# Top-k attention and a Fourier-mix MLP on one core: batch 1's fold in one go, and batch 0's MLP ended before it

## The chip, the cores and the metric

One NeuronCore of a Trainium2 chip runs the whole kernel. The metric is the device time of one execution in microseconds. The kernel before took 2009.99 us, the median of 3 runs (2008.93 to 2011.29).

## What is computed

The reference is cut here to what matters. Attention keeps, in each row of scores, the 32 largest; its output, bridged to (8, 576, 512), goes through a real-valued two-dimensional Fourier transform, a normalisation and an MLP.

```python
# attention: q, k, v are (8, 8, 576, 64), float32
scores = (1 / sqrt(64)) * q @ k.transpose(0, 1, 3, 2)
kth    = np.partition(scores, -32, axis=-1)[..., -32:-31]
scores = np.where(scores >= kth, scores, -1e9)
attn   = softmax(scores)
x      = (attn @ v).transpose(0, 2, 1, 3).reshape(8, 576, 512)

# Fourier mix and MLP: w_ch1 is (512, 2048), w_ch2 is (2048, 512)
mixed = real(fft(fft(x, axis=1), axis=2))
u     = x + mixed
un    = (u - mean(u)) / sqrt(var(u) + 1e-6)
out   = u + maximum(un @ w_ch1, 0) @ w_ch2
```

## The kernel before

The order of all instructions is fixed by a plan in steps. A step stands for one tile of 128 rows of scores of one head (64 rows of two heads in the tail tile): 9 tiles make a pair of heads, 4 pairs a batch, so a batch has 36 steps and the attention 288. In step i, TensorE computes the scores of tile i+3 and transposes the masked exponentials of tile i-2; VectorE finds the 32 largest of tile i in four rounds of MAX8 with three MATCH_REPLACE8 between them, two rounds of tile i beside two of tile i+1; GpSimd and ScalarE build the mask and the exponential.

```python
def top_ops(i, rounds):                       # VectorE; S and wk are tiles of 128 x 576
    for r in rounds:
        src, m8 = s if r == 0 else w, m[:, 8 * r:8 * r + 8]
        nc.vector.max(out=m8, in_=src)
        if r < TOPK // 8 - 1:
            nc.vector.match_replace(w, m8, src, NEG)

def mask(i):
    nc.scalar.activation(out=w, in_=Ssb[i], func=AF.Relu, scale=-FAR, bias=Nt[i][:, 1:2])
    nc.gpsimd.tensor_tensor(out=w, in0=Ssb.pop(i), in1=w, op=ALU.subtract)
```

When the four pairs of a batch are through, its rows x (288 + 288 rows in 5 tiles, the last with 64 tail rows) are folded by symmetry, once for each parity of the frequencies. A fold is a sum or difference of the two halves (first), a fold of the columns (second) and another with a reversed half (third). The 32 tail rows of the second half have to be moved to other partitions first (moved).

```python
def moved():
    out, in_ = place(0)[0:TH, 2, :], x[TH:TAIL, 4, :]
    if eng[1] is nc.vector and eng[0] is nc.vector:
        nc.vector.tensor_copy(out=out, in_=in_)
    else:
        nc.scalar.copy(out=out, in_=in_)

def first(p):      # p 0: 128 x 1024, engine eng[0];  p 1: 32 x 512, engine eng[1], needs moved()
    ...
def second(p):     # two instructions: 128 x 512 (p 0) or 32 x 256 (p 1), engine mid or eng[p]
    ...
def third(n, p):   # two additions each, 128 x 254 (p 0) or 32 x 127 (p 1), engine eng[p]
    ...
```

The buffers of a fold are "own" (two tags, fold_s and fold_d) or the space "hT", which otherwise holds the hidden layer of the MLP. dft_tokens(b, par) is then the transform over the tokens on TensorE, one call for each parity; dft_channels(b, t) that over the channels, one call for each of the 5 tiles; add_mixed (GpSimd), stats and rsqrt (VectorE and GpSimd) and channels_first (transposes) prepare the MLP.

The MLP of a batch is a queue of 68 units of TensorE work: 16 units of the first layer (hidden) for each of two chunks of rows, and 36 of the second layer (back; 4 matmuls of 128 x 512 in the profile's records, lines 771 and 807). The units are spread over the steps up to the time when the next batch's MLP arrives:

```python
def level(i):
    steps = range(i, next((a for a in arrivals if a > i), i + PER_BATCH))
    rest, lev = sum(u[0] for u in queue + held), 0.0
    while lev < 6.4 and sum(max(0.0, lev - fixed_cost(s)) for s in steps) < rest:
        lev += 0.02
    return lev        # planned TensorE time of a step
```

In the main loop a step fills its room up to that level with units. For batch 1 (soon) the plan is:

```python
T0 = end + (2 if first else 3 if soon else 4)          # 74 for batch 1
...
elif soon:
    for par in range(2):
        def folds(par=par, b=b, T1=T0 + 1 + 3 * par):
            f = fold_ops(b, par, (nc.gpsimd, nc.vector), mid=nc.vector)
            at(T1 if par else T1 - 1, "act", f["moved"])
            at(T1, "pool0", lambda: f["first"](0))
            at(T1, "dve", lambda: [
                f["first"](1), f["second"](0), f["second"](1),
                f["third"](0, 1), f["third"](1, 1),
            ])
            at(T1 + 1, "pool0", lambda: [f["third"](n, 0) for n in range(2)])
        at(T0, "begin", folds)
    ft, fc = (T0 + 3, T0 + 6), T0 + 7                   # transforms at 77 and 80, channels from 81
```

Of the kernel before, what the change touches and what calls it, by code (L numbers as in the profile page):

```python
# [59 lines left out]
def kernel(  # L60
# [9 lines left out]
    nc = tc.nc  # L70
# [196 lines left out]
    PER_BATCH = NPB * PER_PAIR  # L267
# [232 lines left out]
    Q1, Q2, Q3 = DM // 4, DM // 2, 3 * DM // 4  # L500
    ROWS3 = (P, P, TH)
    PARTS = [(slice(0, P), slice(0, 2)), (slice(0, TH), slice(2, 3))]
    folded, y_of, yt_of, us_of, rs_of, unT_of = ({} for _ in range(6))

    def fold_ops(b, par, eng, space="own", mid=None):

        x = x_of[b]

        if space == "hT":
            sp = batp.tile([P, NIT * CW[0]], F32, name=f"fsp_{b}", tag="hT")

        def buf(n, name):
            if space == "hT":
                return sp[:, 3 * DM * n:3 * DM * (n + 1)].rearrange("p (s c) -> p s c", s=3)
            pool, tag = (batp, ("fold_s", "fold_d")) if space == "own" else (attp, ("PT0", "PT1"))
            return pool.tile([P, 3, DM], F32, name=f"{name}_{b}_{par}", tag=tag[n % 2], bufs=1)  # L520

        got = folded[b, par] = []

        def place(n):
            while len(got) <= n:
                got.append(buf(len(got), ("sd", "zw", "fg")[len(got)]))
            return got[n]

        def moved():

            out, in_ = place(0)[0:TH, 2, :], x[TH:TAIL, 4, :]
            if eng[1] is nc.vector and eng[0] is nc.vector:
                nc.vector.tensor_copy(out=out, in_=in_)
            else:
                nc.scalar.copy(out=out, in_=in_)

        def first(p):
            sd, op = place(0), ALU.add if par == 0 else ALU.subtract
            if p == 0:
                eng[0].tensor_tensor(out=sd[:, 0:2, :], in0=x[:, 0:2, :], in1=x[:, 2:4, :], op=op)  # L540
            else:
                s_ = sd[0:TH, 2, :]
                eng[1].tensor_tensor(out=s_, in0=x[0:TH, 4, :], in1=s_, op=op)

        def second(p):
            pp, ss = PARTS[p]
            s_, z_ = place(0)[pp, ss], place(1)[pp, ss]
            for cols, op in ((slice(0, Q2), ALU.add), (slice(Q2, DM), ALU.subtract)):
                (mid or eng[p]).tensor_tensor(
                    out=z_[:, :, cols], in0=s_[:, :, 0:Q2], in1=s_[:, :, Q2:DM], op=op  # L550
                )

        def third(n, p):
            pp, ss = PARTS[p]
            z_, f_ = place(1)[pp, ss], place(2)[pp, ss]

            def tt(out, up, down, op):
                eng[p].tensor_tensor(out=f_[:, :, out], in0=z_[:, :, up], in1=z_[:, :, down], op=op)

            if n == 0:  # L560
                eng[p].memset(f_[:, :, Q1:Q1 + 1], 0.0)
                eng[p].tensor_copy(out=f_[:, :, 0:DM:Q2], in_=z_[:, :, 0:DM:Q2])
                up, down = slice(1, Q1), slice(Q2 - 1, Q1, -1)
                tt(up, up, down, ALU.add)
                tt(slice(Q1 + 1, Q2), up, down, ALU.subtract)
            else:
                up, down = slice(Q2 + 1, Q3), slice(DM - 1, Q3, -1)
                tt(up, up, down, ALU.subtract)
                tt(slice(Q3, DM - 1), up, down, ALU.add)
                eng[p].tensor_copy(out=f_[:, :, DM - 1:DM], in_=z_[:, :, Q3:Q3 + 1])  # L570

        return {"moved": moved, "first": first, "second": second, "third": third}

    def fold_steps(f):

        def one():
            f["moved"]()
            f["first"](0)
            f["first"](1)

        def two():
            f["second"](0)
            f["second"](1)

        def three(n):
            f["third"](n, 0)
            f["third"](n, 1)

        return [one, two, lambda: three(0), lambda: three(1)]

    def dft_tokens(b, par):

        while any(u[2] == "hidden" for u in queue):
            one_unit()
        _, zw, fg = folded[b, par]
        if b not in y_of:
            y_of[b] = batp.tile([P, 4, S], F32, name=f"y_{b}", tag="y")
        y = y_of[b]
        yps = [
            ps_m.tile([P, 2, KQ], F32, name=f"yp_{b}_{par}_{g2}", tag="mm") for g2 in range(2)  # L600
        ]

        def mm(g2, gg, st, lhsT, rows, table, start=False):

            nc.tensor.matmul(  # L605
                yps[g2][0:rows, gg, :],
                lhsT=lhsT[0:ROWS3[st]],
                rhs=fs[0:ROWS3[st], table, par, st, :],
                start=start,
                stop=st == 2,  # L610
                skip_group_check=True,
            )

        for g2 in range(2):
            for gg in range(2):
                g = 2 * g2 + gg
                for st in range(2):
                    mm(  # L620
                        g2, gg, st, fg[:, st, P * g:P * (g + 1)], P, gg,
                        start=gg == 0 and st == 0,
                    )
        for st in range(3):
            mm(0, 1, st, zw[:, st, Q1:Q1 + 1], 1, 0)
        for g2 in range(2):
            for gg in range(2):
                g = 2 * g2 + gg
                mm(g2, gg, 2, fg[:, 2, P * g:P * (g + 1)], P, gg)

        mir, back = (
            (slice(HS + 2, S, 2), slice(KQ - 2, 0, -1)) if par == 0
            else (slice(HS + 1, S, 2), slice(KQ - 2, None, -1))
        )
        for g2, yp in enumerate(yps):
            y2 = y[:, 2 * g2:2 * g2 + 2, :]
            nc.scalar.copy(out=y2[:, :, par:HS + 1:2], in_=yp[:, :, 0:KQ - par])
            nc.scalar.copy(out=y2[:, 0, mir], in_=yp[:, 0, back])
            nc.scalar.mul(out=y2[:, 1, mir], in_=yp[:, 1, back], mul=sg[:, g2:g2 + 1])
        if par == 1:  # L640
            tails_of_y(b)
        return 4.3

# [228 lines left out]
    prep("k", 0)  # L872


    plan, costs, arrivals = {}, {}, []

    def at(step, where, fn, cost=0.0):
        plan.setdefault((step, where), []).append(fn)
# [51 lines left out]
    for b in range(B):  # L930
# [3 lines left out]
        T0 = end + (2 if first else 3 if soon else 4)  # L934
        if first:

            def folds(b=b):
                for par, space in ((0, "own"), (1, "hT")):
                    for op in fold_steps(fold_ops(b, par, (nc.vector, nc.vector), space)):
                        op()  # L940
            at(T0, "dve", folds)
            ft, fc = (T0 + 1, T0 + 1), T0 + 1
        elif soon:

            for par in range(2):
                def folds(par=par, b=b, T1=T0 + 1 + 3 * par):
                    f = fold_ops(b, par, (nc.gpsimd, nc.vector), mid=nc.vector)
                    at(T1 if par else T1 - 1, "act", f["moved"])
                    at(T1, "pool0", lambda: f["first"](0))
                    at(T1, "dve", lambda: [  # L950
                        f["first"](1), f["second"](0), f["second"](1),
                        f["third"](0, 1), f["third"](1, 1),
                    ])
                    at(T1 + 1, "pool0", lambda: [f["third"](n, 0) for n in range(2)])
                at(T0, "begin", folds)
            ft, fc = (T0 + 3, T0 + 6), T0 + 7
        elif not last:
            for par in range(2):
                def folds(par=par, b=b, T0=T0):
# [12 lines left out]
            at(ft[par], "pe1", lambda b=b, par=par: dft_tokens(b, par), 4.3)  # L972
        for n, t in enumerate((0, 1, 4, 2, 3)):
            quick = first or last
            s = fc + (0 if first else n // 3 if last else n // 2)
            at(s, "pe2", lambda b=b, t=t, q=quick: dft_channels(b, t, q), 1.75)
            if not quick:
                at(s, "pool2", lambda b=b, t=t: add_mixed(b, t))
                at(s + 1, "dve", lambda b=b, t=t: stats(b, t))
            at(s + (1 if quick else 2), "pe", lambda b=b, t=t: channels_first(b, t), 0.6)  # L980
            if first and t == 4:
                at(s + 1, "pe", lambda: (queue.extend(held), held.clear()) and 0.0)
        at(s + 1, "begin" if quick else "dve", lambda b=b: rsqrt(b))
        arrivals.append(s + (1 if quick else 2))
        at(arrivals[-1], "units", lambda b=b: (queue if b else held).extend(mlp_units(b)))

    queue, held, pending, written, now, out_next = [], [], [], set(), [0], []
    step_us = 6.0
# [12 lines left out]

    def level(i):

        steps = range(i, next((a for a in arrivals if a > i), i + PER_BATCH))
        rest, lev = sum(u[0] for u in queue + held), 0.0
        while lev < 6.4 and sum(max(0.0, lev - fixed_cost(s)) for s in steps) < rest:
            lev += 0.02
# [6 lines left out]
    def one_unit():  # L1014
        c, fn, _ = queue.pop(0)
        fn()
        return c
# [160 lines left out]
```

## Time and profile before

| | |
|---|---|
| span of the profiled execution | 2010.3 us, 27513 instructions |
| TensorE (PE) busy | 1863.9 us, 93% |
| VectorE (DVE) busy | 1641.2 us, 82% |
| ScalarE (ACT) busy | 1220.3 us, 61% |
| GpSimd (POOL) busy | 831.2 us, 41% |
| DMA | 29 GB/s mean |
| attention, steps 0 to 287 | until about 1790 us; then the last batch's transform and MLP |

How to read it: the busy share is an average over stages that differ. Until about 300 us there is no MLP to run and TensorE has gaps; after 1790 us VectorE has nearly nothing to do. Between these, TensorE and VectorE are both busy nearly all the time, so what a stage is bound by has to be read from windows of that stage, and from how far TensorE's step lags behind VectorE's. PEld is the load of weights, beside the matmuls.

### The profile page before, as it was taken

What the parts mean: (1) busy time and instruction counts of PE and PEld (TensorE: products, weight loads), DVE (VectorE), ACT (ScalarE), POOL (GpSimd) and SP (SyncE); (2) the same over time, 40 slices, a digit from 0 to 9 for tenths busy, and PEclk for the clock granted to TensorE, in tenths of its full rate; (3) what the DMA queues carried; (4) which work ended last, traced back from release to release, by engine and by line L of the source; (5) the groups of instructions that cost most, each with busy time, mean ns of one, the idle gap of its engine ahead of it and who ended that gap; (6) DMA issues with size and microseconds to landing.
All of it is one profiled execution on the core that took longest, in us unless ns stands there. A gap on an engine that the chain in (4) does not pass through costs nothing.

```text
span 2010.3 us, 27513 instructions
## 1 busy us (share of the span) xinstructions
PE 1863.9 (93%) x8626; PEld 1126.1 (56%) x8626; DVE 1641.2 (82%) x3405; ACT 1220.3 (61%) x3008; POOL 831.2 (41%) x1114
## 2 busy tenths in 40 slices
PE   5666679999889999999999999999999999998999
PEld 2333356465555656647565656647565656565655
DVE  7999889999999998988889888988899888853100
ACT  6878737677666766656665667656666667541100
POOL 4779822333433365234532374225533364223000
PEclk9678679999999999999999999999999999998999
DMA  4323100010000100001000001010000001000000
GB/s 128 96 82 100 54 7 19 24 26 24 23 19 24 27 24 24 18 18 26 24 24 13 26 19 29 18 32 18 19 24 24 23 15 30 0 14 1 11 14 11
DMA packets 133584, 57.81 MB, mean 29 GB/s; under 512 B 124352, under 2 KB 124480, under 8 KB 133440
## 3 DMA queue, kind: packets, MB, share of 16 engines
q1 hardware_dynamic: 132208, 55.73, 10.3%
q8 instruction: 69, 1.13, 0.2%
q14 instruction: 75, 0.61, 0.1%
q10 hardware_dynamic: 1232, 0.33, 0.1%
HBM read 46.57 MB, written 9.44 MB: 28 GB/s over the span
## 4 chain that ended last, share of the span: by engine, by line
PE 69%; DVE 12%; POOL 6%; ACT 6%; issue 6%; DMA 0%; SPq 0%; POOLq 0%; DVEq 0%
PE cp L771 20%; PE hp L747 20%; PE o L430 7%; PE sp L328 5%; PE tpP L393 5%; DVE m L349 5%; DVE wk L351 4%; PE yp L605 3%; POOL wk L366 3%; PE cp L807 2%; PE mp L661 2%; PE sp_t L298 1%; POOL w L192 1%; ACT wk L365 1%; ACT wk L372 1%
## 5 line engine op out<-in xcount | busy, mean ns | idle before, releaser
L366 POOL TENSOR_TENSOR wk<-S,wk 128x576 f32<-128x576 f32 x288 | 406.9, 1413 | 864.9 <-ACT wk L365 833.6
L349 DVE MAX8 m<-wk 128x8 f32<-128x576 f32 x864 | 623.1, 749 | 5.4
L747 PE MATMUL hp<-unT,w 128*128 128x256 f32 (+1 forms) x2048 | 538.3, 409 | 3.7 <-POOL t L709 2.2
L771 PE MATMUL cp<-w,hT 128*128 128x512 f32 x1024 | 479.3, 600 | 0.0
L747 PEld LDWEIGHTS hp<-unT,w 128*128 128x128 f32 x2048 | 372.7, 190 | 128.2 <-issue 32.2
L351 DVE MATCH_REPLACE8 wk<-m,wk 128x576 f32<-128x576 f32 x576 | 427.6, 742 | 0.0
L771 PEld LDWEIGHTS cp<-w,hT 128*128 128x128 f32 x1024 | 179.6, 190 | 183.6 <-issue 182.8
L372 ACT ACTIVATE wk<-wk,nt 128x576 f32<-128x576 f32 x288 | 225.0, 781 | 79.2 <-POOL wk L366 77.8
L365 ACT ACTIVATE wk<-S,nt 128x576 f32<-128x576 f32 x288 | 226.3, 786 | 50.0 <-POOL nt L358 47.8
L393 PE MATMUL tpP<-ident,wk 128*128 128x128 f32 x1152 | 186.8, 287 | 73.0 <-ACT wk L372 38.0
L396 ACT COPY PT<-tpP 128x512 f32<-128x512 f32 (+1 forms) x320 | 170.7, 544 | 117.4 <-PE tpP L393 114.9
L349 DVE MAX8 m<-S 128x8 f32<-128x576 f32 x288 | 214.1, 743 | 32.8 <-ACT S L302 32.5
L393 PEld LDWEIGHTS tpP<-ident,wk 128*128 128x128 f32 x1152 | 140.3, 146 | 174.2 <-ACT wk L372 56.7
L751 ACT ACTIVATE hT<-hp 128x320 f32<-128x320 f32 (+1 forms) x256 | 104.6, 409 | 192.2 <-PE hp L747 190.0
L351 DVE MATCH_REPLACE8 wk<-m,S 128x576 f32<-128x576 f32 x288 | 213.7, 742 | 0.0
L430 PE MATMUL o<-PT,v 128*64 128x256 f32 (+3 forms) x1440 | 195.9, 414 | 4.6 <-ACT PT L396 4.1
L331 ACT COPY S<-sp 128x512 f32<-128x512 f32 (+1 forms) x264 | 141.9, 588 | 73.3 <-PE sp L328 73.0
L328 PE MATMUL sp<-kT,qT 64*128 64x512 f32 (+1 forms) x528 | 168.1, 690 | 2.3 <-ACT means L922 1.9
L430 PEld LDWEIGHTS o<-PT,v 128*64 128x64 f32 x1440 | 111.5, 153 | 78.1 <-issue 14.6
L192 POOL TENSOR_TENSOR w<-w,space 128x512 f32<-128x512 f32 x96 | 123.6, 1287 | 8.6 <-ACT space L183 5.7
L785 DVE SCALAR_TENSOR_TENSOR x<-cp,gi,x 128x512 f32<-128x512 f32 x11 | 8.2, 746 | 128.3 <-PE cp L771 128.3
L479 DVE TENSOR_TENSOR x<-tpx,rd 128x256 f32<-128x256 f32 x64 | 27.1, 424 | 73.7 <-PE tpx L475 71.0
(125 smaller groups left out, 1899.0 us busy)
## 6 DMA issues: line engine op xcount, KB each, us to landing
space<-in_moe_w_ch_dram SPq DMA_DIRECT2D x32, 512.0 KB, 3.5
nat<-in_q_dram SPq DMA_DIRECT2D x128, 64.0 KB, 2.0
v<-in_v_dram SPq DMA_DIRECT2D x128, 64.0 KB, 2.1
out_dram<-x SPq DMA_DIRECT2D x32, 256.0 KB, 2.1
nat<-in_k_dram SPq DMA_DIRECT2D x124, 64.0 KB, 2.1
nat<-in_q_dram SPq DMA_DIRECT2D x128, 8.0 KB, 1.7
v<-in_v_dram SPq DMA_DIRECT2D x128, 8.0 KB, 1.7
nat<-in_k_dram SPq DMA_DIRECT2D x124, 8.0 KB, 1.7
```

The source lines that it names most:

```text
L192: nc.gpsimd.tensor_tensor(out=dst, in0=dst, in1=(low, high, ex)[part], op=ALU.mult if part else ALU.add,)
L328: nc.tensor.matmul(sp[r], lhsT=qT[hd, q_cols], rhs=kT[hd, :], start=True, stop=True)
L349: ops.append(lambda src=src, m8=m8: nc.vector.max(out=m8, in_=src))
L351: ops.append(lambda src=src, m8=m8: nc.vector.match_replace(w, m8, src, NEG))
L365: nc.scalar.activation(out=w, in_=Ssb[i], func=AF.Relu, scale=-FAR, bias=Nt[i][:, 1:2])
L366: nc.gpsimd.tensor_tensor(out=w, in0=Ssb.pop(i), in1=w, op=ALU.subtract)
L372: nc.scalar.activation(out=w, in_=w, func=AF.Exp, bias=Nt.pop(i)[:, 0:1], accum_out=den_t[pair % 3][:, c:c + 1],)
L393: nc.tensor.transpose(tp[:, c, :], p_sb[:, k0 + P * c:k0 + P * (c + 1)], ident)
L396: nc.scalar.copy(out=pt[:, NF * he:NF * (he + 1), col:col + w], in_=tp[:, :, o:o + w])
L430: nc.tensor.matmul(o[D * e:D * (e + 1), c0:c1], lhsT=vv[:, c, e, :], rhs=pt[:, 2 * NF if c == NF else NF * e + c, c0:c1], start=(c == 0), ...
L747: nc.tensor.matmul(hp[:, 0:w], lhsT=w1[:, dt, P * it:P * (it + 1)], rhs=unT[:, dt, 0:w], start=(dt == 0), stop=(dt == NDT - 1),)
L771: nc.tensor.matmul(cp, lhsT=hT[:, it, P * n:P * (n + 1)], rhs=w2[:, it, :], start=(it == 0), stop=(it == NIT - 1),)
```

## The change

It touches the stage around batch 1's fold, some 40 steps on each side of step 74.

- Batch 1's two parities are folded in one go from step 74: parity 1 wholly on VectorE, in the hT space; parity 0 in step 75, shared with GpSimd as before. Their token transforms stand at steps 76 and 77, the channel transforms at 78 and 79.
- For that, hT has to be free at step 74: batch 0's MLP is spread over the steps up to 74 (a new list, ends, takes the place of arrivals in level), and what is left of it is emptied at the start of that step.
- Batch 1's MLP starts at step 80, with the first chunk of rows, instead of 85.
- moved() is always on ScalarE. This concerns both folds of batch 0 and one of the last batch; the others had it there already.
- The tails of y are taken when both parities are done, whichever comes last.

The purpose is to close the stretch around batch 1's fold in which TensorE has too little to do.

The diff, cut to its core:

```diff
         def moved():
             out, in_ = place(0)[0:TH, 2, :], x[TH:TAIL, 4, :]
-            if eng[1] is nc.vector and eng[0] is nc.vector:
-                nc.vector.tensor_copy(out=out, in_=in_)
-            else:
-                nc.scalar.copy(out=out, in_=in_)
+            nc.scalar.copy(out=out, in_=in_)
...
         if first:
-            def folds(b=b):
+            def folds(b=b, T0=T0):
                 for par, space in ((0, "own"), (1, "hT")):
-                    for op in fold_steps(fold_ops(b, par, (nc.vector, nc.vector), space)):
-                        op()
-            at(T0, "dve", folds)
+                    f = fold_ops(b, par, (nc.vector,) * 2, space)
+                    at(T0, "act", f["moved"])
+                    for op in fold_steps(f, False):
+                        at(T0, "dve", op)
+            at(T0, "begin", folds)
...
         elif soon:
-            for par in range(2):
-                def folds(par=par, b=b, T1=T0 + 1 + 3 * par):
-                    ...
-            ft, fc = (T0 + 3, T0 + 6), T0 + 7
+            def folds(b=b, T0=T0):
+                while queue:
+                    one_unit()
+                f = [
+                    fold_ops(b, 0, (nc.gpsimd, nc.vector), "own", nc.vector),
+                    fold_ops(b, 1, (nc.vector,) * 2, "hT"),
+                ]
+                for n in (1, 0):
+                    at(T0, "act", f[n]["moved"])
+                for op in fold_steps(f[1], False):
+                    at(T0, "dve", op)
+                at(T0 + 1, "pool0", lambda: f[0]["first"](0))
+                at(T0 + 1, "dve", lambda: [
+                    f[0]["first"](1), f[0]["second"](0), f[0]["second"](1),
+                    f[0]["third"](0, 1), f[0]["third"](1, 1),
+                ])
+                at(T0 + 2, "pool0", lambda: [f[0]["third"](n, 0) for n in range(2)])
+            at(T0, "begin", folds)
+            ft, fc = (T0 + 3, T0 + 2), T0 + 4
...
-            s = fc + (0 if first else n // 3 if last else n // 2)
+            s = fc + (0 if first else n // 3 if soon or last else n // 2)
...
-            if first and t == 4:
-                at(s + 1, "pe", lambda: (queue.extend(held), held.clear()) and 0.0)
+            if (first or soon) and t == 4:
+                ready = s + (1 if first else 2)
+                at(ready, "pe", lambda: (queue.extend(held), held.clear()) and 0.0)
...
-        arrivals.append(s + (1 if quick else 2))
-        at(arrivals[-1], "units", lambda b=b: (queue if b else held).extend(mlp_units(b)))
+        arrivals.append(ready if first or soon else s + (1 if quick else 2))
+        at(arrivals[-1], "units", lambda b=b: (queue if b > 1 else held).extend(mlp_units(b)))
+        ends.append(T0 if soon else arrivals[-1])
...
     def level(i):
-        steps = range(i, next((a for a in arrivals if a > i), i + PER_BATCH))
+        steps = range(i, next((a for a in ends if a > i), i + PER_BATCH))
```

More of the change, by code (lines that the diff above doesn't have):

```diff
@@ L502 @@
     PARTS = [(slice(0, P), slice(0, 2)), (slice(0, TH), slice(2, 3))]
-    folded, y_of, yt_of, us_of, rs_of, unT_of = ({} for _ in range(6))
+    folded, y_of, done_of, yt_of, us_of, rs_of, unT_of = ({} for _ in range(7))
     def fold_ops(b, par, eng, space="own", mid=None):
@@ L572, in fold_ops, with fold_steps @@
         return {"moved": moved, "first": first, "second": second, "third": third}
-    def fold_steps(f):
+    def fold_steps(f, moved=True):
         def one():
-            f["moved"]()
+            if moved:
+                f["moved"]()
             f["first"](0)
@@ L639, in dft_tokens @@
             nc.scalar.mul(out=y2[:, 1, mir], in_=yp[:, 1, back], mul=sg[:, g2:g2 + 1])
-        if par == 1:
+        done_of.setdefault(b, set()).add(par)
+        if len(done_of[b]) == 2:
             tails_of_y(b)
@@ L872 @@
     prep("k", 0)
-    plan, costs, arrivals = {}, {}, []
+    plan, costs, arrivals, ends = {}, {}, [], []
     def at(step, where, fn, cost=0.0):
@@ L935 @@
         if first:
-            def folds(b=b):
+            def folds(b=b, T0=T0):
                 for par, space in ((0, "own"), (1, "hT")):
-                    for op in fold_steps(fold_ops(b, par, (nc.vector, nc.vector), space)):
-                        op()
-            at(T0, "dve", folds)
+                    f = fold_ops(b, par, (nc.vector,) * 2, space)
[3 more added lines that the diff above has]
+            at(T0, "begin", folds)
             ft, fc = (T0 + 1, T0 + 1), T0 + 1
         elif soon:
-            for par in range(2):
-                def folds(par=par, b=b, T1=T0 + 1 + 3 * par):
[L947 to L955, printed above, removed]
-            ft, fc = (T0 + 3, T0 + 6), T0 + 7
+            def folds(b=b, T0=T0):
[17 more added lines that the diff above has]
+            ft, fc = (T0 + 3, T0 + 2), T0 + 4
         elif not last:
```

## The prediction

> **What bounds the kernel now.** I read the shares of busy time first, then the groups, then the windows cut at the edges of the plan's steps, then the timelines of VectorE, TensorE and GpSimd around batch 1's fold. From the page:
>
> ```profile
> PE 1863.9 (93%) x8626; PEld 1126.1 (56%) x8626; DVE 1641.2 (82%) x3405; ACT 1220.3 (61%) x3008; POOL 831.2 (41%) x1114
> ...
> L349 DVE MAX8 m<-wk 128x8 f32<-128x576 f32 x864 | 623.1, 749 | 5.4
> ...
> L351 DVE MATCH_REPLACE8 wk<-m,wk 128x576 f32<-128x576 f32 x576 | 427.6, 742 | 0.0
> ```
>
> TensorE looks like the bound for the whole span. But each step of the plan needs four MAX8 and three MATCH_REPLACE8 on VectorE; these seven with their value loads take 5.08 us, the distance from one tile's first MAX8 on S to the next tile's in an undisturbed stretch of VectorE's timeline (316.7 to 321.8 us). So the question is which engine bounds the steps that the change touches. I take the start of a step as that first MAX8: step 39 starts at 298.5, step 74 at 487.5, step 80 at 531.5, step 85 at 563.5, step 123 at 769.5, step 127 at 799.9. Busy time between these edges (columns: stretch, length, PE, PEld, DVE, ACT, POOL, granted clock, DMA):
>
> ```profile
> 298.50:487.50 189.00, 186.65 (x898) 111.64 (x900) 183.05 (x379) 132.22 (x332) 61.41 (x87) 1.00 0.10 23
> 487.50:531.50 44.00, 38.66 (x179) 22.05 (x175) 43.50 (x90) 25.69 (x67) 22.34 (x29) 0.92 0.08 20
> 531.50:563.50 32.00, 29.35 (x164) 20.82 (x165) 31.38 (x72) 22.26 (x54) 13.02 (x16) 1.00 0.07 19
> 563.50:769.50 206.00, 199.66 (x938) 116.37 (x938) 199.04 (x408) 137.47 (x349) 88.76 (x131) 0.98 0.10 23
> 769.50:799.90 30.40, 27.56 (x169) 19.67 (x168) 25.99 (x60) 23.76 (x63) 14.39 (x17) 1.00 0.15 36
> ```
>
> In the second and third rows, batch 1's fold and transform, TensorE idles 5.3 + 2.7 us while VectorE idles 0.5 + 0.6: VectorE is the bound there. In the first row VectorE idles 6.0 of 189.0, and 2.5 of that is the 0.07 us that every step loses. Only from batch 2 on does TensorE bound: over steps 163 to 198 (1018.6 to 1240.9) it is busy 220.6 of 222.3 us and VectorE 193.7.
>
> VectorE's timeline at batch 0's two folds:
>
> ```profile
> 267.80 3.15 DVE L549 TENSOR_TENSOR zw<-sd 128x512 f32<-128x512 f32 x4
> ...
> 276.91 1.95 DVE L549 TENSOR_TENSOR fsp<-fsp 128x512 f32<-128x512 f32 x4
> ```
>
> and at the first of batch 1's:
>
> ```profile
> 499.18 3.17 DVE L549 TENSOR_TENSOR zw<-sd 128x512 f32<-128x512 f32 x4
> ```
>
> The same four instructions take 1.95 us alone and 3.15 to 3.17 when a GpSimd subtraction (1.4 to 2.1 us, in GpSimd's timeline at 268.2 and 499.6) lies beside them. And the largest bubble of TensorE here, in its timeline, at step 86:
>
> ```profile
> 571.36 1.11 PE L393 MATMUL tpP<-ident,wk 128*128 128x128 f32 x4 [5.62 <-ACT kT L257]
> ```
>
> GpSimd's timeline shows what lies behind it: the sixteen small instructions of rsqrt run from 563.0 to 567.3, and the mask's subtraction of step 84 stands behind them, then the exponential, then this transpose.
>
> **What the Trainium skill says.** "Perfetto Trace Analysis", section "Identifying the Most-Contended Engine", calls a busy share of matmuls a poor measure and occupancy a fair one for VectorE; the five windows agree, since TensorE at 97% (199.66 of 206.00) goes with steps of 5.1 us set by VectorE. "SBUF — State Buffer", section "Who interferes with whom", says that a tensor_tensor with both inputs in SBUF contends with GpSimd for a shared port and that the loser blocks; the 1.95 against 3.15 us agree. "TensorE: Matmul & The Clock Gate", Part 1, says that the clock halves after an idle stretch; the trace grants 0.50 in step 86, during the bubble shown above, and 0.92 over the second window.
>
> **The change part by part.** First a yardstick. The plan's own unit costs give TensorE 169.0 us for steps 40 to 72; its first score matmul of step 40 starts at 307.8 and that of step 73 at 480.2, 172.4 us. For steps 88 to 121 it is 183.4 against 187.1. So TensorE needs 1.02 times the plan's costs when nothing holds it.
>
> *Batch 0's MLP ends by step 72 instead of 78.* Before, 28 matmul records of line 771 follow 487.5 in TensorE's timeline: 7 units of 4 records, at 3.44 us per 8 about 12 us. The change moves them ahead of step 74. Followed step by step, the plan gives TensorE 184.8 us for steps 40 to 72, so TensorE starts step 73 at 307.8 + 184.8 x 1.02 = 496.3, 16.1 later. Before, TensorE began step 73 2.1 us ahead of VectorE (480.2 against 482.4): VectorE set the pace. Where TensorE does (steps 136 to 155), its scores start some 3 us behind VectorE's step. So VectorE starts step 73 near 493.3, **10.9 us later**. This is the cost of the change.
>
> *The folds of batch 1.* Before, VectorE's parts of the two take 5.8 (498.58 to 504.39) and 5.7 us (519.50 to 525.18), the rest is GpSimd's. After, parity 0 stays so (5.8); parity 1 is all VectorE's, as batch 0's second fold: 275.17 to 281.22, 6.05 us without the copy, and one meeting with a GpSimd subtraction, 1.2, so 7.3. Sum 13.1 against 11.5: **1.6 us more on VectorE**. TensorE, with 6.4 planned us for steps 73 to 75, idles through these folds by some 15 us, where it had seven MLP units to do before. The transforms then stand at steps 76 to 79 instead of 77 to 83.
>
> *Batch 1's MLP over steps 80 to 121 instead of 85 to 121.* The same work over five more steps: the plan's level falls from 5.42 to 5.06, so TensorE no longer holds VectorE up. What VectorE can win there is its idle time above 0.07 a step: 7.0 - 2.7 = 4.3 us in steps 85 to 122 and 4.4 - 0.3 = 4.1 in 123 to 126. **8.4 us less**, of which I leave 1 as still lost.
>
> *The copies on ScalarE.* Batch 0: VectorE saves two copies of 0.41 us. But ScalarE is at line 365 until 268.1 in that step and the copies stand behind it, so the first small fold instruction waits to about 268.7, where it stood at 267.2; in return zw no longer meets the GpSimd subtraction. Net 0.2 later. Batch 7: the copy's 0.44 us lie on the chain at 1819.58, but the next instruction there (1820.02, 3.26 us where batch 0's took 1.23) ends with GpSimd's own, so 0 to 1 us comes off; I take 0.3.
>
> *The sum.* VectorE takes 317.5 us from step 73 to step 127 (482.4 to 799.9). After: 493.3 + 317.5 + 1.6 - 7.4 = 805.0, 5 us later. There batch 2's rsqrt stands, and TensorE resumes about 9.1 us behind it (563.5 to 572.6 for batch 1), at 814.1 with step 129; before, that step began at 811.2. From there the program is the same and TensorE bounds it: 2.9 + 0.2 - 0.3 = 2.8, so 2010.0 + 2.8, about **2012.5**.
>
> **The rivals.** *TensorE's idle time is the loss, and the change removes it.* TensorE needs 273.9 planned us from step 73 to 127, x 1.02 = 279.4, so it could stand at 496.3 + 279.4 = 775.7 instead of 795.3, where it starts step 127 before: up to 19 us less, about 1991. For it speaks 93% busy; against it, that VectorE has no slack there: 483.0 busy of 501.4 us between steps 39 and 127. The change adds to that and takes nothing away, so 6 to 10 us is the most I believe. *A new wait at the fold*: parity 1 lies in hT's space, so it must wait for the last matmul on hT and for ScalarE's copy. In the new order the last unit stands two steps ahead and the copy right behind the mask of tile 73, so I see none; each step lost there would cost 5 us, 2018. *More meetings of GpSimd and VectorE*: each costs 1.2 us; three more make 2016.
>
> **Range and chances.** The least sure terms are the 3 us of lag (2 to 4.5), the 8.4 us won back (4 to 8.4) and the meetings (0 to 3 of 1.2 us). Together, with the first rival at part strength, 2003 to 2019. Two per cent is 40 us, beyond all rivals: within 2% at 0.98, each side 0.01.
>
> **What would show it.** Right: VectorE starts step 73 near 493 and idles some 10 us more between steps 39 and 73; TensorE idles over 10 us during the fold; parity 1's fold takes 7 us or a little more; VectorE idles little between steps 80 and 123; step 127 starts near 805. Wrong: VectorE's step 73 still near 482 (TensorE had slack that I don't see), TensorE busy through the fold, a wait of VectorE on ScalarE's copy in step 74, or a gain of over 8 us.

## The result: 10 us slower, and the profile after

The changed kernel takes 2021.55 us (median of 6 runs, 2017.37 to 2023.89) against 2011.43 for the kernel before in the same session: ratio 1.0049, 95% interval 1.0034 to 1.0065. Within 2%, as predicted, but not within the range of 2003 to 2019: slower by three to four times the predicted 2.8 us. The six runs lie in two groups of three, 2017.4 to 2019.5 and 2023.6 to 2023.9, and the profiled one is of the second; what parts the groups isn't shown.

The shares of busy time say nothing of it, since all engines do nearly the same work as before:

```profile
PE 1872.6 (93%) x8626; PEld 1130.9 (56%) x8626; DVE 1646.3 (81%) x3410; ACT 1222.4 (60%) x3011; POOL 827.6 (41%) x1106
```

The windows, cut at the same steps (39, 74, 80, 85, 123, 127) as in the prediction, show where the time went. The columns are again stretch, length, PE, PEld, DVE, ACT, POOL, granted clock, DMA:

```profile
294.50:496.70 202.20, 198.31 (x918) 117.90 (x920) 183.82 (x379) 131.27 (x330) 61.28 (x87) 0.99 0.10 23
496.70:546.20 49.50, 38.88 (x209) 26.86 (x205) 48.87 (x102) 29.30 (x75) 23.34 (x28) 0.86 0.07 18
546.20:575.50 29.30, 24.55 (x124) 16.15 (x124) 28.50 (x65) 17.31 (x44) 10.91 (x26) 0.94 0.05 11
575.50:779.70 204.20, 197.44 (x935) 113.85 (x933) 200.98 (x409) 139.54 (x356) 88.17 (x119) 0.99 0.10 23
779.70:809.30 29.60, 27.11 (x166) 19.18 (x165) 26.00 (x61) 22.89 (x59) 12.99 (x16) 1.00 0.15 37
```

Length against before: +13.2, +5.5, -2.7, -1.8, -0.8 us. In the first row VectorE now idles 18.4 us (202.20 - 183.82), 12.4 more than before. In the second and third it is busy 77.37 of 78.80 us, so the fold there is VectorE work. In the fourth its busy time rose, from 199.04 to 200.98, where less time was to be lost.

Most of the rise in the second row is in one place. VectorE's timeline of the changed kernel at parity 1's fold, and at parity 0's behind it:

```profile
501.93 2.27 DVE L537 TENSOR_TENSOR fsp<-x 128x1024 f32<-128x1024 f32 x1
504.12 0.67 DVE L540 TENSOR_TENSOR fsp<-x,fsp 32x512 f32<-32x512 f32 x1
504.73 5.29 DVE L546 TENSOR_TENSOR fsp<-fsp 128x512 f32<-128x512 f32 x4
...
519.00 1.95 DVE L546 TENSOR_TENSOR zw<-sd 128x512 f32<-128x512 f32 x4
```

and GpSimd's timeline over the same time:

```profile
501.72 1.40 POOL L366 TENSOR_TENSOR wk<-S,wk 128x576 f32<-128x576 f32 x1 [4.82 <-ACT wk L365]
...
505.14 2.12 POOL L366 TENSOR_TENSOR wk<-S,wk 128x576 f32<-128x576 f32 x1 [0.89 <-ACT wk L365]
507.23 2.52 POOL L537 TENSOR_TENSOR sd<-x 128x1024 f32<-128x1024 f32 x1
```

The four instructions of line 546 take 1.95 us alone, as at 519.00. At 504.73 they meet two GpSimd instructions in a row, a mask's subtraction and parity 0's first sum, and take 5.29. Parity 1's first difference, at 501.93, meets a third and takes 2.27. The prediction allowed for one meeting of 1.2 us. The Trainium skill ("SBUF — State Buffer", "Who interferes with whom") says that a VectorE instruction with two inputs in SBUF contends with a GpSimd instruction that reads SBUF, and calls the shared port an exclusive lock; the trace agrees, with 5.29 us against 1.95. The two chains end at 510.02 and 509.75.

For the whole, the table gives the length of stages between starts of VectorE's steps, in us, from each kernel's trace. (The changed kernel's profiled run was 2.1 us ahead at step 36, before anything that the change touches; lengths are free of that.)

| stage, steps | before | changed | e2_spread | e4_head | v2_late_flush | v3 | e7_spread80 |
|---|---|---|---|---|---|---|---|
| 36 to 39 | 44.9 | 43.1 | 41.8 | 43.1 | 43.0 | 42.9 | 44.9 |
| 39 to 73 | 183.9 | 196.6 | 196.6 | 196.6 | 187.0 | 187.0 | 185.6 |
| 73 to 85 | 81.1 | 84.4 | 81.9 | 83.4 | 85.0 | 84.0 | 81.2 |
| 85 to 123 | 206.0 | 204.2 | 207.9 | 202.2 | 201.8 | 201.9 | 205.2 |
| 123 to 127 | 30.4 | 29.6 | 27.4 | 29.9 | 29.6 | 29.5 | 27.4 |
| 127 to 286 | 977.5 | 977.5 | 976.5 | 978.3 | 977.5 | 975.5 | 976.5 |
| 286 to the end | 232.8 | 235.3 | 236.6 | 236.2 | 232.6 | 232.6 | 232.7 |

### The profile page after: what moved, and what is told of

It reads as the page before. It is cut to its first block, busy times and chain, and to the rows that moved or that the text cites. A ratio compares the mean times of both kernels' runs of the same rounds, so it can differ in the third digit from the quotient of the medians.

```text
span 2022.1 us, 27519 instructions
## 1 busy us (share of the span) xinstructions
PE 1872.6 (93%) x8626; PEld 1130.9 (56%) x8626; DVE 1646.3 (81%) x3410; ACT 1222.4 (60%) x3011; POOL 827.6 (41%) x1106
## 4 chain that ended last, share of the span: by engine, by line
PE 69%; DVE 14%; POOL 6%; issue 6%; ACT 5%; DMA 0%; POOLq 0%; SPq 0%; DVEq 0%; ACTq 0%
PE cp L770 20%; PE hp L746 19%; PE o L430 7%; DVE m L349 6%; PE sp L328 5%; PE tpP L393 5%; DVE wk L351 5%; PE yp L603 3%; PE cp L806 2%; PE mp L660 2%; POOL wk L366 2%; PE sp_t L298 1%; POOL w L192 1%; ACT wk L365 1%; PE cm L911 1%
## 5 line engine op out<-in xcount | busy, mean ns | idle before, releaser
L349 DVE MAX8 m<-S 128x8 f32<-128x576 f32 x288 | 214.0, 743 | 30.3 <-ACT S L302 29.9
L358 POOL TENSOR_TENSOR nt<-m,cc 128x2 f32<-128x2 f32 x288 | 56.6, 197 | 87.2 <-DVE m L349 87.2
```

The source lines that it names most:

```text
L349: ops.append(lambda src=src, m8=m8: nc.vector.max(out=m8, in_=src))
```

## The experiments

**Which part costs it: the copies, or the spread MLP?** Two kernels, each the kernel before with one part of the change. In e1_copies moved() is on ScalarE, as in the diff above. In e2_spread only the plan of batch 0's MLP changes:

```diff
+        ends.append(T0 if soon else arrivals[-1])
...
-        steps = range(i, next((a for a in arrivals if a > i), i + PER_BATCH))
+        steps = range(i, next((a for a in ends if a > i), i + PER_BATCH))
```

> The kernel before with one part of the change alone: the tails' rows of batch 0 (both folds) and of batch 7 are moved by ScalarE. In the two profiles, steps 37 and 38 took 39.0 us before and 37.3 after the change. Theory 1 (the copies save VectorE time on a stretch that nothing else covers): 1 to 2 us faster than before, near 2009.8. Rival, the prediction's own step (VectorE waits for ScalarE and gains nothing): 0 to 0.3 us slower. In the profile, steps 37 and 38 together tell: 37.3 or 39.2.

> The kernel before with another part alone: batch 0's MLP is spread to step 74 instead of 85 (level 5.62 for 5.14), everything else as before, the folds of batch 1 too. Theory 1 (the early MLP makes TensorE the bound in steps 39 to 73, and VectorE, which sets the pace of the steps up to 127, never gets that time back): VectorE begins step 73 11 to 13 us later, and the whole is 9 to 13 us slower than before, 2021 to 2024. Theory 2 (the fold on VectorE is the loss): within 2 us of before.

Measured: e1_copies 2013.78 us, ratio 1.0004 (0.9996 to 1.0012), no difference. e2_spread 2025.6 us, 1.0062 (1.0049 to 1.0074): this part alone costs most of what the change costs. Counted from step 36 to step 286, e2_spread is 8.2 us behind the kernel before and the changed kernel 11.5. The further 3.7 us by which its profiled run is longer come after step 286, where its program is that of before (last section), so that its larger total is the spreading's isn't shown. In the table its 39 to 73 is the changed kernel's 196.6. The window of that stage of e2_spread (its VectorE is busy 178.22 us and so idles 18.4):

```profile
292.80:489.40 196.60, 194.19 (x895) 115.90 (x894) 178.22 (x370) 127.67 (x323) 59.40 (x86) 0.99 0.09 22
```

In e1_copies VectorE waits for ScalarE's copy in front of the small fold instruction, as its timeline has it, and then meets no GpSimd subtraction in zw:

```profile
268.93 1.34 DVE L540 TENSOR_TENSOR sd<-x,sd 32x512 f32<-32x512 f32 x1 [1.97 <-ACT sd L532]
270.20 1.94 DVE L546 TENSOR_TENSOR zw<-sd 128x512 f32<-128x512 f32 x4
```

Counted from step 36, the fold's last VectorE instruction ends 0.5 us later than before. Steps 37 and 38 still take 37.1 us, the figure of theory 1. The copies are not the reason, as e2_spread, with its copies as before, has 36.1. It goes with the granted clock behind the fold: from 280 to 284 us it is 0.50 before and 1.00 in e1_copies and e2_spread. In e1_copies it falls later. TensorE's windows, first of the kernel before, then of e1_copies:

```profile
284.00:288.00 4.00, 3.99 (x20) 0.85 0.00 0
...
300.00:304.00 4.00, 4.00 (x16) 1.00 0.00 0
```

```profile
284.00:288.00 4.00, 3.99 (x21) 1.00 0.02 4
...
300.00:304.00 4.00, 4.00 (x12) 0.71 0.00 0
```

Step 40 then takes 9.7 us and not 8.0, so that at step 41 e1_copies is only 0.3 us ahead.

**Is the loss proportional to what is spread?** e7_spread80 is e2_spread with a later end, so that TensorE gets only 3.5 us more of plan before step 73, not 15.8:

```diff
-        ends.append(T0 if soon else arrivals[-1])
+        ends.append(T0 + 6 if soon else arrivals[-1])
```

> The kernel before with batch 0's MLP spread evenly up to step 80 (the plan's costs of steps 40 to 72 add up to 172.5 us, against 169.0 before and 184.8 in the changed kernel); batch 1 as before. Theory: TensorE is 1.02 x 3.5 = 3.6 us later at step 73, and the 3 to 5 us by which it ran ahead of VectorE take most of it up: VectorE reaches step 73 0 to 2 us later and the whole is within 2 us of before. Rival: every us of plan counts from the first on, VectorE is 3.6 us later at step 73 and the whole 3 us slower, 2015.

Measured: 2008.8 us, 0.9993 (0.9982 to 1.0004), no difference from before; 12 of its 17 runs lie at 2006.3 to 2009.1 and 5 at 2016.0 to 2017.4, and why is open. VectorE reaches step 73 1.8 us later. Counted from step 41 on, where the difference in clock is past, 3.5 us of plan made TensorE 2.9 us longer and cost VectorE 1.8; the next 12.3 us (to e2_spread's 184.8) made it 10.7 longer and cost 9.2. So the loss is not proportional: slack takes up more of the first piece than of the second, without a sharp end.

**How much of the fold is GpSimd's doing?** e4_head is the changed kernel with parity 0's first sum on VectorE in step 75; it takes the 2.52 us GpSimd instruction away from parity 1's fold.

```diff
-                at(T0 + 1, "pool0", lambda: f[0]["first"](0))
                 at(T0 + 1, "dve", lambda: [
-                    f[0]["first"](1), ...
+                    f[0]["first"](0, nc.vector), f[0]["first"](1), ...
```

> The changed kernel, with parity 0's first sum of batch 1 (128 x 1024) on VectorE in step 75 instead of GpSimd, where it ran beside parity 1's fold and held it up. Theory 1 (blocking at the shared port): step 74 falls from 16.3 us by 2 to 3, step 75 grows by 1.1 to 1.2; 1 to 2 us faster than the changed kernel, about 2020. Rival (the sum on GpSimd costs VectorE nothing): step 74 stays at 16 us and the whole is 1 us slower.

Measured: 2018.46 us, 1.0037 (1.0023 to 1.0051). This interval overlaps that of the changed kernel (1.0034 to 1.0065), so a gain in the whole time isn't shown; the trace shows the part. VectorE's timeline of e4_head:

```profile
502.76 2.27 DVE L537 TENSOR_TENSOR fsp<-x 128x1024 f32<-128x1024 f32 x1
...
505.56 3.15 DVE L546 TENSOR_TENSOR fsp<-fsp 128x512 f32<-128x512 f32 x4
```

The second line falls from 5.29 to 3.15, so 2.1 us were that one meeting. What remains are two meetings with mask subtractions, one of them in the 2.27. Step 75 becomes 1.1 us longer for the sum it took over, so steps 73 to 85 gain 1.0 of the 2.1.

**Where is the time that should come back at steps 85 to 126?** Of the 8.4 us that I counted as idle there, 2.6 came back (1.8 + 0.8 in the table). The largest piece left is a wait of VectorE at step 123, on a buffer that TensorE's transposes of tile 120 must free. VectorE's timeline, first of the kernel before, then of the changed one:

```profile
774.49 0.09 DVE L351 MATCH_VALUE_LOAD wk<-m,S 128x8 f32 x1 [3.50 <-PE tpP_t L404]
```

```profile
784.18 0.09 DVE L351 MATCH_VALUE_LOAD wk<-m,S 128x8 f32 x1 [3.04 <-PE tpP_t L404]
```

My first theory was that batch 2's token transform, which stands ahead of these transposes in TensorE's order, causes it. e6_behind is the changed kernel with the transforms of batches 2 to 6 behind the transposes; v6 is the kernel before with the same edit:

```diff
-            at(ft[par], "pe1", lambda b=b, par=par: dft_tokens(b, par), 4.3)
+            at(ft[par], "pe1" if first or soon or last else "pe9", lambda b=b, par=par: dft_tokens(b, par), 4.3)
...
             fixed.append(lambda: transposes(done))
+        fixed += plan.pop((i, "pe9"), [])
```

> The changed kernel, with one thing moved: the token transforms of the folds of batches 2 to 6 stand behind the step's transposes in TensorE's order, not ahead of them. My theory: the wait of 3.0 us at step 123, where VectorE's MATCH_VALUE_LOAD waits for the transposes of tile 120, was put there by the transform, and it goes: steps 123 to 127 shrink from 29.6 us to about 27, and as VectorE sets the pace up to there the end comes 2 to 4 us earlier, near 2017 to 2019. Rival: TensorE bounds from step 127 on whatever VectorE does, the wait only moves to a later step, and the time stays within 1 us of the changed kernel's 2021.

> The kernel before with the token transforms of batches 2 to 6 behind the step's transposes and nothing else. Theory: the wait of 3.5 us at step 123 goes and 2 to 4 us with it, 2008 to 2010; rival: no difference, 2012.

Measured: e6_behind 2020.17 us, 1.0042 (1.0029 to 1.0054), and v6 2009.09, 0.9987 (0.9979 to 0.9994). The wait at step 123 is gone, but steps 123 to 127 take 30.2 us in e6_behind against 29.6: other waits stand in its place one and two steps later. VectorE's timeline of e6_behind:

```profile
790.53 0.69 DVE L688 BATCH_NORM_STATS2 st<-x 128x6 f32<-128x512 f32 x1 [0.98 <-POOL x L683]
...
792.85 0.69 DVE L688 BATCH_NORM_STATS2 st<-x 128x6 f32<-128x512 f32 x1 [1.41 <-POOL x L683]
...
799.57 0.17 DVE L457 TENSOR_SCALAR rd<-den 128x6 f32<-128x6 f32 x1 [0.88 <-ACT den L449]
```

So the order was not the cause; my theory falls. The small gain of both lies elsewhere: steps 127 to 163 take 217.4 us, not 218.7, and steps 163 to 199 and 235 to 271 0.9 us less each; steps 271 to 286 give 1.0 back.

The second theory starts from TensorE's side. At step 113 the changed kernel's TensorE leads VectorE by 6.4 us (before, it was 2.0 behind), yet at step 119 it is 1.1 behind. In between lies batch 2's fold on GpSimd. Two kernels ask whether that fold takes the lead away or TensorE's own work does. e8_no_fold2 leaves the fold of batch 2 out, and its transforms read the rows x as they are; e9_half_tokens2 leaves out 8 of the 15 matmuls in each of batch 2's token transforms. Neither computes the whole of what the reference asks.

```diff
# e8_no_fold2
-            for par in range(2):
+            for par in range(2 if b > 2 else 0):
                 def folds(par=par, b=b, T0=T0):
...
-        _, zw, fg = folded[b, par]
+        _, zw, fg = (None, x_of[b], x_of[b]) if b == 2 else folded[b, par]
# e9_half_tokens2
-                for st in range(2):
+                for st in range(1 if b == 2 else 2):
```

> The changed kernel without the fold of batch 2: GpSimd's 20 or so operations of it (some 9 us for each parity, in steps 113 to 122) and ScalarE's two copies are left out, and the token transforms of batch 2 read the unfolded rows, so TensorE has the same matmuls. Under the theory that GpSimd's fold delays the mask subtractions, with them the exp and TensorE's transposes, and so takes away TensorE's lead of 6 us in steps 113 to 119: TensorE still leads by 4 us or more at step 119, the wait of 3.0 us at step 123 is gone, and steps 123 to 127 take 26 to 27 us, not 29.6. Rival, that TensorE's own work of these steps (transforms and MLP) is more than VectorE's: the lead at step 119 is 1 to 2 us at most and the wait stays above 2 us.

> The changed kernel with the token transforms of batch 2 leaving out their second row group, 8 of the 15 matmuls of each parity, about 2.3 us of TensorE each; the order of everything else as it was. Theory of TensorE's own work: 4.6 us less on TensorE before step 123, so the wait of 3.0 us there is gone and the end comes some 3 us earlier. Rival, GpSimd's fold sets TensorE's pace in steps 113 to 119: the wait shrinks by less than 1.5 us, as only the second transform (step 122) counts at most by half.

Measured: at step 119 TensorE leads by 2.0 us in e8_no_fold2 and is 0.2 behind in e9_half_tokens2. Without the fold there is no wait at step 123 and steps 123 to 127 take 27.0 us. With half the transforms the wait shrinks by 1.7 us and the stage takes 27.9; VectorE's timeline of e9_half_tokens2:

```profile
781.74 0.09 DVE L351 MATCH_VALUE_LOAD wk<-m,S 128x8 f32 x1 [1.34 <-PE tpP_t L404]
```

So both have a part, and GpSimd's is the larger of the two; neither expectation was met in full. Of the 7.5 us of lead that go in steps 113 to 119, 3.1 go with the fold and 0.9 with the half transforms; the rest stays open. Nor is the wait these two alone: e2_spread and e7_spread80, with fold and transforms whole, take 27.4 us for steps 123 to 127. (e8_no_fold2 also won 1.7 us on the changed kernel between steps 85 and 105, ahead of the fold, where its phase against GpSimd is another; that is not the fold's.) What the fold does is seen in GpSimd's timeline of the changed kernel. The small line 358, from which a tile's mask starts, stands behind the fold's pieces:

```profile
736.67 0.85 POOL L555 TENSOR_TENSOR fg<-zw 32x127 f32<-32x127 f32 x2
737.49 0.18 POOL L358 TENSOR_TENSOR nt<-m,cc 128x2 f32<-128x2 f32 x1
738.56 1.41 POOL L366 TENSOR_TENSOR wk<-S,wk 128x576 f32<-128x576 f32 x1 [0.89 <-ACT wk L365]
```

In e8_no_fold2 this subtraction starts at 736.57. VectorE is 0.9 us earlier there too, so the fold delays this mask by 1.1 us. The delay grows over the next tiles: 2.9 us two tiles on, and 6.7 three tiles further, reckoned in the same way. TensorE meets it as longer waits for the exponential (line 372), here in its timelines, first of the changed kernel and then of e8_no_fold2:

```profile
735.96 0.66 PE L393 MATMUL tpP<-ident,wk 128*128 128x128 f32 x4 [1.95 <-ACT wk L372]
```

```profile
733.85 0.66 PE L393 MATMUL tpP<-ident,wk 128*128 128x128 f32 x4 [0.77 <-ACT wk L372]
```

The whole time of e8_no_fold2 is hardly better all the same, 2021.13 us (2020.13 to 2022.17), and e9_half_tokens2 took 2022.74 us (2020.59 to 2025.08). Taken from step 36 on, e8_no_fold2 is 4.8 us ahead of the changed kernel at step 127 and 2.7 ahead at step 163. TensorE's windows behind step 127 show what took the difference (stretch, length, PE busy, clock, DMA). First e8_no_fold2:

```profile
799.40:803.50 4.10, 0.71 (x10) 0.90 0.19 42
803.50:806.50 3.00, 2.96 (x8) 0.50 0.00 0
806.50:809.50 3.00, 3.00 (x10) 0.50 0.00 0
```

then the changed kernel at the same place:

```profile
805.00:807.30 2.30, 0.69 (x9) 1.00 0.29 63
807.30:810.30 3.00, 2.99 (x15) 1.00 0.04 8
```

As TensorE came earlier, it waited longer for VectorE's last rows (3.43 us in its timeline, not 1.62), and after that wait the clock was half for 6 us: some 3 us of full speed lost, of the order of the 2.1 us that went. The Trainium skill ("TensorE: Matmul & The Clock Gate", "Part 1") puts the fall to half rate at an idle window of some 3.4 us; the two waits here lie on either side of that.

**Is there a version that is faster?** v2_late_flush takes the good parts: copies on ScalarE, batch 0's MLP not spread to step 74 but emptied at step 76, parity 0 folded first with GpSimd and parity 1 wholly on VectorE a step later, batch 1's MLP from step 81. v3 is v2_late_flush with the edit of e6_behind, and v7 is e7_spread80 with that edit. The core of v2_late_flush against the kernel before:

```diff
+            at(T0 + 2, "begin", folds1)        # empties the MLP queue, then parity 1 on VectorE, in hT
+            ft, fc = (T0 + 3, T0 + 4), T0 + 5
-            ft, fc = (T0 + 3, T0 + 6), T0 + 7
...
+        ends.append(T0 + 11 if soon else arrivals[-1])
```

> The early start of batch 1's MLP without the early end of batch 0's: parity 0 is folded in step 75 as before, parity 1 wholly on VectorE in hT's space in step 76; batch 0's MLP is spread as before (level 5.10), and its last 4 units run at the start of step 76, while VectorE folds; batch 1's MLP arrives at step 81; copies on ScalarE. Theory 1 (the spreading is the loss): the 11 us of steps 39 to 73 vanish; against before 1.7 less for batch 0, 1.6 more for the fold, 2.6 less in steps 85 to 127: near 2008.7, and 10 us or more faster than the changed kernel. Theory 2 (the fold on VectorE, or the early MLP of batch 1, is the loss): 2015 or more.

> The version v2_late_flush (copies on ScalarE, parity 0's fold early, parity 1's wholly on VectorE, batch 1's MLP from step 81, batch 0's MLP not spread) with the token transforms of batches 2 to 6 behind the step's transposes. If the wait at step 123 is real work for the path, 2007 to 2009, 0.998 of before; if it is slack of TensorE's, 2010 to 2011 as v2_late_flush.

> The kernel before with two small things: batch 0's MLP spread to step 80 (as e7_spread80) and the token transforms of batches 2 to 6 behind the step's transposes (as v6). Each alone measured 2009 against 2012. If the gains are of different stretches they add up: 2005 to 2007. If both only remove the same wait, 2008 to 2009.

Measured: v2_late_flush 2010.39 us, 0.9993 (0.9985 to 1.0001); v3 2007.44, 0.9978 (0.9969 to 0.9986); v7 2012.66, 1.0006 (0.9997 to 1.0016). v3 is faster than both kernels of the case, by 0.2% than the one before. v7 shows that gains of this size don't add up: its two parts gave 0.9993 and 0.9987 alone. Counted from step 36 to step 286, v7 gains 1.6 us on the kernel before, e7_spread80 3.0 and v6 2.7; behind step 286 v7's profiled run takes 235.3 us, theirs 232.6 to 232.7. In v2_late_flush the stretch 36 to 127 takes 546.5 us against 546.3 before: steps 85 to 123 take 4.2 us less, steps 39 to 85 7.0 more. No run separates its parts, so what an MLP that starts four steps earlier brings by itself isn't shown.

## Why the prediction was right and wrong

The sign and the mechanism of the cost held; the step that failed is the sum, in three of its terms: what the folds cost (1.6 us, measured 3.3), what comes back behind them (7.4 us, measured 2.6), and how much of VectorE's delay reaches TensorE (all but 2.2 us, measured all of it).

- *"VectorE starts step 73 near 493.3, 10.9 us later"*: right in the number, in part by luck. Counted from step 36 on it is 10.9 later, and 9.6 in e2_spread with this part alone. But two errors of the working cancel. TensorE took 186.1 us for steps 40 to 72 (305.50 to 491.61), 1.007 times the planned 184.8 and not 1.02 times: 2.4 us less. And it stood 0.5 us behind VectorE's step 73 (491.09), not 3. The start of step 73 in TensorE's timeline of the changed kernel:

```profile
491.61 0.66 PE L313 MATMUL sp<-kT,qT 64*64 64x256 f32 x8
```

- *"1.6 us more on VectorE"* for the folds: too small. Parity 1 took 10.45 us (501.93 to 512.38), not 7.3, since it met GpSimd three times and one of these was the change's own placing of parity 0's sum. Steps 73 to 85 grew by 3.3 us: 1.7 missed, as VectorE's other work there took some 2 us less. The rival of more meetings named this.
- *"8.4 us less, of which I leave 1 as still lost"*: the largest miss. 2.6 came back (1.8 + 0.8), where 7.4 was counted and 4 was my lower end: 4.8 missed. Two things were wrong. First, less idle isn't less time when other operations grow. Avoidable idle in 85 to 122 did fall from 4.3 us to below 1, but VectorE's busy time rose by 1.9. One such operation in the groups of the stretch, before and then changed:

```profile
L822 DVE SCALAR_TENSOR_TENSOR x<-ct,gi,x 64x512 f32<-64x512 f32 x1 | 0.7, 746 | 0.0
```

```profile
L821 DVE SCALAR_TENSOR_TENSOR x<-ct,gi,x 64x512 f32<-64x512 f32 x1 | 1.8, 1832 | 0.0
```

  In e4_head and v2_late_flush, with another phase against GpSimd, the stretch took 202.2 and 201.8 us, which is the 4 us I had counted; the same operation took 1.34 and 0.74 us there. Second, the wait at step 123 wasn't a want of TensorE's time over the whole stretch but of steps 113 to 123: the lead that the lighter plan gave TensorE was gone by step 119, and e8_no_fold2 shows GpSimd's fold as the larger of the two causes tried.
- *"TensorE resumes about 9.1 us behind it ... 2.9"*: wrong. I took the 9.1 from batch 1's rsqrt, where TensorE's wait at step 86 ended with ScalarE's copy of kT, 1.7 us after the exponential that I named. For batch 2 TensorE starts step 129 11.2 us behind VectorE's step 127 in the trace of before (811.17 against 799.93), and 11.2 in the changed kernel (820.50 against 809.27). TensorE's timelines, in this order:

```profile
811.17 0.49 PE L298 MATMUL sp_t<-kt,qT 128*128 128x128 f32 x2
```

```profile
820.50 0.49 PE L298 MATMUL sp_t<-kt,qT 128*128 128x128 f32 x2
```

  So nothing is swallowed: TensorE inherits the whole delay of VectorE, not 2.2 us less.
- The three terms add up: 2.9 + 1.7 + 4.8 + 2.2 = 11.6, and less the 2.1 us by which the profiled run was ahead, 9.5; VectorE's step 127 shows 9.4 (809.3 against 799.9). It stays so up to step 286 (977.5 us from 127 in both); the other 2.5 us between the two profiled runs come after it. (2010.0 + 2.8 is 2012.8, not 2012.5.)
- *"Net 0.2 later"* for the copies: near in size (0.5 at the end of the fold in e1_copies), but the clock behind it, which I hadn't counted, leaves step 41 0.3 us earlier. *"I take 0.3"* for batch 7 isn't seen, because the end varies by more: 232.8 us before and 235.3 after.
- *"TensorE's idle time is the loss, and the change removes it"*: no. TensorE still idles 10.6 us in steps 74 to 79 (38.88 busy of 49.50), as said of the fold, and VectorE, not TensorE, sets the pace up to step 127. *"A new wait at the fold"*: none for the hT space or the copy there.

## What to carry to other kernels

Where two engines have nearly the same load, as here in steps 39 to 73, work moved to the other side of a stage costs less while slack takes it up and most of its time beyond that (1.8 of TensorE's first 2.9 us, then 9.2 of 10.7). It can be estimated ahead of time: planned work times its yardstick, less the slack. What should come back on the other side needs its own proof: ask of every idle microsecond which wait it is, what stands next in line behind it, and which engine takes the lead away again. A delay's passage from one engine to another is best read from the same batch of the kernel before, not from a neighbour.

## What was not expected of the hardware

The end of the kernel is not one number. After the last fold TensorE starts at half clock, and how long it stays there differs from kernel to kernel. TensorE's windows of before and then of the changed kernel at the start of the last batch's transform:

```profile
1834.40:1838.40 4.00, 4.00 (x15) 0.52 0.00 0
1838.40:1842.40 4.00, 4.00 (x15) 1.00 0.00 0
```

```profile
1847.80:1851.80 4.00, 4.00 (x11) 0.50 0.00 0
1851.80:1855.80 4.00, 4.00 (x9) 0.86 0.00 0
```

Half clock lasts some 6 us before and in v2_late_flush, and 12 to 14 us in the changed kernel, e1_copies, e2_spread and e4_head. Steps 286 to the end take 232.6 to 232.8 us in the first two and 235.3 to 236.6 in the other four, with the same program there but for one copy. What decides it no run here settles; it is of the size of the differences that this case is about, and 2.5 us of it lie between the two profiled runs. Counted only from step 36 to step 286, e1_copies is 0.4 us faster than the kernel before, v2_late_flush 0.1 slower, v6 2.7, e7_spread80 3.0 and v3 3.1 faster, so the last three gains do not come from the end.
